# Lightning attention and a gated feed-forward layer on one core: two iotas and two additions for four small iotas, and 96 bytes of padding ahead of the tiles of q, k and v

## The chip, the core and the metric

The kernel runs on one core of a Trainium2 chip. A core has TensorE (PE; its weight loads are listed apart as PEld), VectorE (DVE), ScalarE (ACT), GpSimd (POOL) and SyncE (SP), each with its own instruction stream, and 16 DMA engines that they share. The metric is the device time of one execution in microseconds (us), the median over several runs; less is better.

## The reference

Inputs: `q`, `k`, `v` of shape (4, 8, 768, 64), eight decay factors `lam` between 0.97 and 0.99, and three weight matrices; all are float32. Linear attention with decay runs over blocks of 64 positions, and its output goes through a gated feed-forward layer:

```python
for b in range(nb):                       # 12 blocks of 64
    qb, kb, vb = q[:, :, sl], k[:, :, sl], v[:, :, sl]
    intra = einsum('bhic,bhjc->bhij', qb, kb) * Dmask        # lam ** (i - j), zero for j > i
    intra = einsum('bhij,bhjd->bhid', intra, vb)
    inter = einsum('bhid,bhde->bhie', qb * lam ** (i + 1), kv_state)
    out[:, :, sl] = intra + inter
    kv_state = lam ** 64 * kv_state + einsum('bhsd,bhse->bhde', kb * lam ** (63 - s), vb)

x = out.transpose(0, 2, 1, 3).reshape(3072, 512)
y = (sigmoid(x @ w_gate) * (x @ w_val)) @ w_out              # 512 -> 1536 -> 512
```

## The kernel before

The 768 positions are taken in six steps `n` of 128. In each step all four batches and eight heads are worked on: attention gives `XT[n]`, the transposed input of the feed-forward layer, 512 tokens wide; twelve slices `ft` of 128 hidden columns follow (`piece_gv`: products `gp` and `vp` at L484, the sigmoid at L496, the product `ht` at L499 or L501), and then four output tiles of 128 tokens (`piece_po`, L519). The attention of step n+1 is put between the slices of step n, so TensorE has the dense products to do while other engines prepare. The order on each engine is the order of the code.

Attention of step 0 has nothing to hide behind. It needs k of batches 0 and 1 (`load_hw`, issued by SP as float32 and cast at L289), the rest of k, q and v (`load`, L94, issued by POOL, float32 in memory and bf16 in the tile), transposes on TensorE (L263), products S = K Q (`piece_s`, L306), a mask (`piece_m`, L314) and products with v (`piece_a`, L337 and L580). Between them stand matrix products of zeros (L533) that nothing reads.

Memory is laid out in the order in which tiles are made, pool after pool, each tile on a multiple of 32 bytes: constants first (the weights `WG`, `WV`, `WO`, then the small tables), then the pool `qkv` (4 buffers of k, 4 of q, 5 of v, 4,096 bytes per partition each), then all others: the float32 tiles of `load_hw`, the transposed `qt` and `kt`, `kd`, `KS` and `QS`, `MT`, `XT`, `sg`, `ht`, `ob`, `st`, `xd`. The last constant is `gates` (L607), two bf16 values per partition. It ends the constants so that the first buffer of k starts at byte 64,544, which is 504 x 128 + 32; the sizes of all later tiles are multiples of 1,024, so that each of them stands 32 bytes past a multiple of 128. The weights start at byte 16,512, a multiple of 128, and so do the large masks and `lamq2`.

POOL issues the loads of q, k, v and weights, and makes the small tables between the first of them. One of these is `jn` (L132), two float32 values per partition. With s the row within a half of 64 partitions, column 0 holds -1 - s and column 1 holds 63 - s. They are filled by four iotas at L174, one for each half and column. ACT takes them as scales: `tables_late` (L217) makes `pk` (L218) and `kds` (L219), powers of `lam`, from them. `tri` (L176) follows the iotas on POOL, then the loads of q for batches 2 and 3, of v in three parts, and of the weights, slice by slice.

From step 2 on, q and k are transposed by DMA (`xbar`, L294, issued by SP). `next_loads` (L613) orders it: the two transposes, then `gate` (L609), two copies on POOL of one column of `qt` and `kt` into `gates`, which hold POOL back until both transposes have landed, then the load of v for this step and of q and k for the next. For step 2 the loads of q and k are issued by L605 and the v load by `next_loads(2)`; TensorE first reads that v in `chunk_c` (L443), behind slice 8 of step 1.

Of the kernel before, what the change touches and what calls it, by code (L numbers as in the profile page):

```python
# [9 lines left out]
BF16 = mybir.dt.bfloat16  # L10
# [6 lines left out]
def kernel(  # L17
# [11 lines left out]
    nc = tc.nc  # L29

    B, H, S, D = q.shape
    C = 128
# [9 lines left out]
    const = ctx.enter_context(tc.tile_pool(name="const", bufs=1))  # L42
# [18 lines left out]
    L = C // 2  # L61
# [20 lines left out]
    def rows_of(u):  # L82
        return slice(u * 64, (u + 1) * 64)

    def load(n, what, b0=0, b1=B):
        sl = slice(n * C, (n + 1) * C)
        for c in what:
            if (c, n) not in T_:
                T_[c, n] = qkv.tile([128, B, H, D], BF16, tag=c + "b", name=c + "b",
                                      bufs=5 if c == "v" else 4)  # L90
            src = {"q": q, "k": k, "v": v}[c]
            nat = b1 if n == 0 or c == "v" else min(b1, NB2)
            if b0 < nat:
                nc.gpsimd.dma_start(  # L94
                    out=T_[c, n][:, b0:nat],
                    in_=src[b0:nat, :, sl, :].rearrange("b h s d -> s (b h) d"))
            if nat < b1:
                m = max(nat, b0)
                for u in range(2):
                    nc.gpsimd.dma_start(  # L100
                        out=T_[c, n][:, m:b1, u::2, :],
                        in_=src[m:b1, 1 - u::2, sl, :].rearrange("b h s d -> s (b h) d"))
# [29 lines left out]
    jn = const.tile([128, 2], FP32, tag="jn")  # L132
# [31 lines left out]
    for u in range(2):  # L164
# [4 lines left out]
                            pattern=[[1, C]], channel_multiplier=-1)  # L169
    nc.gpsimd.iota(ip1, pattern=[[1, C]], base=1, channel_multiplier=0,  # L170
                   allow_small_or_imprecise_dtypes=True)
    load(0, "k", 2, 4)
    for u, i, base in ((0, 0, -1), (1, 0, -1), (0, 1, L - 1), (1, 1, L - 1)):
        nc.gpsimd.iota(jn[rows_of(u), i:i + 1], pattern=[[0, 1]], base=base, channel_multiplier=-1,  # L174
                       allow_small_or_imprecise_dtypes=True)
    nc.gpsimd.affine_select(out=tri, in_=tri, compare_op=ALU.is_gt, fill=1.0, base=0,  # L176
                            pattern=[[-1, C]], channel_multiplier=1)
# [35 lines left out]

    def powers(u):
        nc.scalar.activation(mask0[:, u], mask0[:, u], AF.Exp)

    def tables_late():  # L217
        nc.scalar.activation(pk[:, 1], lnl, AF.Exp, scale=jn[:, 0:1])  # L218
        nc.scalar.activation(kds[:, 1], lnl, AF.Exp, scale=jn[:, 1:2])  # L219
        nc.scalar.activation(pow_l, lns, AF.Exp, scale=float(L))  # L220
# [38 lines left out]
    def t_(c, n, bs, pool=ps_at, tag="ps"):  # L259
        ps = pool.tile([128, len(bs), HP, C], BF16, name="t" + c, tag=tag)  # L260
        for i, b in enumerate(bs):
            for hp in range(HP):
                nc.tensor.transpose(ps[:, i, hp, :], T_[c, n][:, b, 2 * hp:2 * hp + 2, :], ident)  # L263
        (tqs if c == "q" else tks)[n, bs[0]] = ps

    def e_q(n, bs, eng=None):
        w = len(bs)
        src = tqs[n, bs[0]] if n < FIRST_XBAR else QT[n][:, bs[0]:bs[0] + w]
        t = trsb.tile([128, 2, HP, C], BF16, tag="QS", name="QS")
        if n == 0:  # L270
            (nc.scalar.copy if eng is nc.scalar else nc.vector.tensor_copy)(t[:, :w], src)
        else:
            nc.vector.tensor_tensor(
                out=t[:, :w], in0=src,
                in1=(lamqs if swapped(n, bs[0]) else lamq).unsqueeze(1).to_broadcast([128, w, HP, C]),
                op=ALU.mult)
        for i in range(w):
            QS[n, bs[i]] = t[:, i]
# [252 lines left out]
    def zeros(m):  # L531
        for _ in range(m):
            nc.tensor.matmul(zps, lhsT=ST[1, 0][:, 0, 0], rhs=ST[1, 0][:, 0], start=True, stop=True)  # L533

    zeros(9)
    exponents(0)
    powers(0)
    cast_hw("k", 0)
    t_("k", 0, [0])
    e_k(0, [0])  # L540
    exponents(1)
    cast_hw("k", 1)
    zeros(3)
    powers(1)
    t_("q", 0, [0])
    e_q(0, [0], nc.vector)
    t_("q", 0, [1])
# [56 lines left out]
    load(1, "v", 2, 4)  # L604
    load(2, "qk")  # L605

    gates = const.tile([128, 2], BF16, tag="gates")  # L607

    def gate(n):  # L609
        for i, t in enumerate((QT[n], KT[n])):  # L610
# [157 lines left out]
```

## Time and profile before

| | |
|---|---|
| median of six runs | 226.27 us (226.12 to 227.44) |
| profiled execution | 225.77 us |
| its span on the core | 224.0 us |
| granted TensorE clock | 1.0 throughout |
| first product with weights (L484) | at 15.84 us |
| last product (L519) | 221.0 us |

The profile is of one execution, on its own time. Busy time by stretch of the span, in us, from a table of windows:

| stretch | TensorE | DVE | ACT | POOL | DMA, GB/s written |
|---|---|---|---|---|---|
| 0 to 5.7 | 4.02 | 2.67 | 3.06 | 4.35 | 113 |
| 5.7 to 8.1 | 1.47 | 1.46 | 1.93 | 2.34 | 150 |
| 8.1 to 12 | 3.26 | 2.90 | 2.89 | 3.90 | 127 |
| 12 to 17 | 4.58 | 4.40 | 3.59 | 5.00 | 168 |
| 17 to 60 | 42.73 | 24.41 | 23.60 | 23.21 | 176 |
| 60 to 78 | 17.31 | 13.42 | 10.02 | 7.84 | 151 |
| 78 to 205 | 126.84 | 51.65 | 57.20 | 17.74 | 91 |
| 205 to 224 | 15.97 | 3.31 | 4.04 | 0 | 57 |

TensorE is the busy engine from 17 us to the end; POOL is busy nearly all the time up to 17 us, mostly with issuing loads. A part of the groups of instructions (line, engine, operation, tiles, shape, count, then busy us, mean ns of one, idle time ahead and what ended it):

```profile
L484 PE MATMUL gp<-XT,WG 128*128 128x512 bf16 (+1 forms) x296 | 74.2, 374 | 0.1
L519 PE MATMUL po<-WO,ht 128*128 128x512 bf16 (+2 forms) x292 | 63.3, 370 | 0.5 <-issue 0.2
L611 POOL COPY gates<-qt 128x1 bf16<-128x1 bf16 x4 | 0.7, 186 | 49.1 <-DMA qt<-qb 49.1
L314 DVE TENSOR_TENSOR MT<-sp,mask 128x512 bf16<-128x512 f32 x16 | 9.9, 684 | 2.7 <-PE sp L306 2.7
```

The means of the first two mix shapes; with the shapes apart both are 379 ns for 128x512. Matrix products overlap in the pipeline: four of 128x512 follow each other in 0.865 us. The transposes of L294 land between 5.5 and 10.1 us after their issue for `qt`, and 4.3 to 5.0 for `kt`.

### The profile page before, as it was taken

How to read it: one execution, taken by the hardware profiler on the slowest of the kernel's cores; microseconds unless marked ns; L12 is line 12 of the kernel's file. 1: busy time of each engine (PE TensorE's matmuls, PEld its weight loads, DVE VectorE, ACT ScalarE, POOL GpSimd, SP SyncE). 2: the span in 40 equal slices, each digit the busy share in tenths (PEclk: the TensorE clock that was granted, in tenths of full speed). 3: DMA queues.
4: the chain of work that ended last, by engine and by line, in shares of the span. 5: the costliest groups of instructions: out<-in, count | busy, mean ns of one | idle time of the engine just before them, and what ended most of it. 6: DMA issues, size and time to landing. Idle time of an engine off the chain costs nothing.

```text
span 224.0 us, 5200 instructions
## 1 busy us (share of the span) xinstructions
PE 216.2 (97%) x2178; PEld 106.3 (47%) x2187; DVE 104.2 (47%) x194; ACT 106.3 (47%) x232; POOL 64.4 (29%) x85
## 2 busy tenths in 40 slices
PE   7799999999998999999999999999999999999994
PEld 2454444557444544444544444544444544444443
DVE  4686653539776700686700676700676400333300
ACT  5777534494385433376342366342367342333221
POOL 7999864760075000940291012000000000000000
PEclk9999999999999999999999999999999999999999
DMA  7999999999969999999599989212100012100022
GB/s 112 136 164 183 195 201 180 177 155 147 176 52 157 234 128 151 198 156 153 113 105 209 212 139 81 15 50 94 47 3 0 0 52 94 47 0 0 4 94 95
DMA packets 106009, 25.25 MB, mean 113 GB/s; under 512 B 97153, under 2 KB 103553, under 8 KB 105985
## 3 DMA queue, kind: packets, MB, share of 16 engines
q0 software_dynamic: 82944, 13.90, 84.2%
q1 hardware_dynamic: 22752, 10.95, 22.9%
q8 instruction: 17, 0.28, 0.6%
q10 hardware_dynamic: 288, 0.07, 0.1%
q14 instruction: 8, 0.06, 0.1%
HBM read 28.32 MB, written 6.29 MB: 154 GB/s over the span
## 4 chain that ended last, share of the span: by engine, by line
PE 67%; DMA 19%; POOL 8%; issue 2%; SPq 1%; ACT 0%; POOLq 0%
PE po L519 23%; PE gp L484 20%; PE vp L484 20%; DMA WO<-in_moe_w_out_dram 6%; DMA qb<-in_q_dram 4%; DMA WV<-in_moe_w_val_dram 4%; DMA vb<-in_v_dram 3%; POOL WV L108 2%; POOL WG L105 2%; DMA kt<-kb 2%; SPq L294 1%; POOL vb L94 1%; PE cp L443 1%; PE op L407 1%; PE op L421 1%
## 5 line engine op out<-in xcount | busy, mean ns | idle before, releaser
L484 PE MATMUL gp<-XT,WG 128*128 128x512 bf16 (+1 forms) x296 | 74.2, 374 | 0.1
L484 PE MATMUL vp<-XT,WV 128*128 128x512 bf16 (+1 forms) x292 | 74.1, 376 | 0.0
L496 ACT ACTIVATE sg<-gp 128x512 bf16<-128x512 f32 x72 | 43.0, 597 | 63.1 <-PE gp L484 63.1
L501 DVE TENSOR_TENSOR ht<-sg,vp 128x512 bf16<-128x512 bf16 x48 | 33.0, 687 | 79.9 <-PE vp L484 77.0
L519 PE MATMUL po<-WO,ht 128*128 128x512 bf16 (+2 forms) x292 | 63.3, 370 | 0.5 <-issue 0.2
L484 PEld LDWEIGHTS <-WV 128*128 128x128 bf16 x292 | 28.6, 98 | 33.4 <-DMA WV<-in_moe_w_val_dram 0.2
L519 PEld LDWEIGHTS <-ht 128*128 128x128 bf16 x300 | 28.3, 98 | 31.8
L484 PEld LDWEIGHTS <-WG 128*128 128x128 bf16 x296 | 28.1, 98 | 31.8 <-DMA WG<-in_moe_w_gate_dram 0.8
L523 ACT COPY ob<-po 128x512 f32<-128x512 f32 (+1 forms) x24 | 13.7, 572 | 38.9 <-PE po L519 38.9
L127 ACT ACTIVATE kd<-kb,kds 128x128 bf16<-128x128 bf16 (+1 forms) x88 | 28.8, 401 | 0.0
L499 DVE TENSOR_TENSOR ht<-sg,vp 128x512 bf16<-128x512 bf16 x24 | 16.5, 687 | 13.2 <-PE vp L484 13.2
L611 POOL COPY gates<-qt 128x1 bf16<-128x1 bf16 x4 | 0.7, 186 | 49.1 <-DMA qt<-qb 49.1
L94 POOL DMA_DIRECT2D vb<-in_v_dram x9 | 11.9, 1333 | 2.8 <-issue 1.7
L314 DVE TENSOR_TENSOR MT<-sp,mask 128x512 bf16<-128x512 f32 x16 | 9.9, 684 | 2.7 <-PE sp L306 2.7
L433 ACT CAST XT<-op 128x512 bf16<-128x512 f32 x16 | 8.2, 599 | 5.0 <-PE op L421 5.0
L393 DVE TENSOR_TENSOR MT<-sp,mask 128x512 bf16<-128x512 f32 x16 | 10.3, 682 | 0.0
L100 POOL DMA_DIRECT2D qb<-in_q_dram x10 | 8.8, 895 | 3.5 <-DMA WO<-in_moe_w_out_dram 3.2
L94 POOL DMA_DIRECT2D qb<-in_q_dram x8 | 8.8, 1105 | 1.7 <-POOLq L752 0.8
L100 POOL DMA_DIRECT2D kb<-in_k_dram x10 | 9.0, 917 | 1.0 <-DMA WG<-in_moe_w_gate_dram 0.6
L533 PE MATMUL zps<-st 128*128 128x512 bf16 x17 | 6.7, 530 | 1.6 <-DVE st L159 1.5
L108 POOL DMA_DIRECT2D WV<-in_moe_w_val_dram x9 | 7.3, 822 | 0.3 <-DMA WG<-in_moe_w_gate_dram 0.3
L94 POOL DMA_DIRECT2D kb<-in_k_dram x6 | 7.1, 1176 | 0.6 <-DMA WG<-in_moe_w_gate_dram 0.5
(79 smaller groups left out, 115.4 us busy)
## 6 DMA issues: line engine op xcount, KB each, us to landing
out_dram<-ob SPq DMA_DIRECT2D x19, 256.0 KB, 2.1
vb<-in_v_dram POOLq DMA_DIRECT2D x4, 512.0 KB, 7.3
qb<-in_q_dram POOLq DMA_DIRECT2D x6, 256.0 KB, 8.2
kb<-in_k_dram POOLq DMA_DIRECT2D x6, 256.0 KB, 10.7
qb<-in_q_dram POOLq DMA_DIRECT2D x12, 128.0 KB, 8.3
WO<-in_moe_w_out_dram POOLq DMA_DIRECT2D x4, 384.0 KB, 12.2
kb<-in_k_dram POOLq DMA_DIRECT2D x10, 128.0 KB, 10.7
WG<-in_moe_w_gate_dram POOLq DMA_DIRECT2D x4, 256.0 KB, 7.3
```

Of the source, the lines that this page charges most:

```text
L94: nc.gpsimd.dma_start(out=T_[c, n][:, b0:nat], in_=src[b0:nat, :, sl, :].rearrange("b h s d -> s (b h) d"))
L100: nc.gpsimd.dma_start(out=T_[c, n][:, m:b1, u::2, :], in_=src[m:b1, 1 - u::2, sl, :].rearrange("b h s d -> s (b h) d"))
L108: nc.gpsimd.dma_start(out=WV[:, :, f0 * 128:f1 * 128], in_=wv_r[:, :, f0 * 128:f1 * 128])
L127: nc.scalar.mul(KD[n][:, at, i, :], T_["k", n][:, at, i, :], kds[:, min(n // FIRST_XBAR, 1), h:h + 1])
L314: nc.vector.tensor_tensor(out=MT[n, b][:, u], in0=SP[n, b][u], in1=mask0[:, 1 - u if swapped(n, b) else u], op=ALU.mult)
L393: nc.vector.tensor_tensor(out=MT[n, bp][:, u], in0=SP[n, bp][u], in1=mask[:, u ^ bp].unsqueeze(1).to_broadcast([128, 2, HP, L]), op=ALU.mult)
L484: nc.tensor.matmul(ps[:, part], lhsT=W[:, mt, fs], rhs=XT[n][:, part, mt], start=(part is not second and mt == 0), stop=(part is not first ...
L496: nc.scalar.activation(sg, gp.rearrange("p a b -> p (a b)"), AF.Sigmoid)
L499: mul = nc.vector.tensor_mul(HT[n, ft], sg, vp.rearrange("p a b -> p (a b)"))
L501: mul = nc.vector.tensor_mul(HT[n, ft].rearrange("p (b c i) -> p c b i", b=B, c=2), sg.rearrange("p (c b i) -> p c b i", c=2, b=B), vp.rea ...
L519: nc.tensor.matmul(po[:, :c1 - c0], lhsT=HT[n, ft][:, tt * 128:(tt + 1) * 128], rhs=WO[:, ft, c0:c1], start=(ft == 0), stop=(ft == NFT - 1))
L523: (eng.copy if eng is nc.scalar else eng.tensor_copy)(o, po[:, :c1 - c0])
```

## The change

The tile `gates` is made 64 bf16 values wide, 128 bytes in place of 4; its use stays as it was. Everything behind it moves by 96 bytes, so that the first buffer of k starts at byte 64,640, which is 505 x 128, and all later tiles on multiples of 128 as well (each 128 bytes past a multiple of 256).

The four iotas for `jn` become two over all 128 partitions, one for each column, with the values -1 - p and 127 - p for partition p. That is right for column 0 in the first half and for column 1 in the second. Two additions on VectorE put the other halves right: +64 to column 0 in partitions 64 to 127, and -64 to column 1 in partitions 0 to 63 (`chunk_rows`). They stand in VectorE's order behind the cast of batch 1's k and ahead of the copy of the transposed q (L271 before). ACT's readers of `jn` wait for them in place of POOL. No other instruction changes its place on any engine.

```diff
-    for u, i, base in ((0, 0, -1), (1, 0, -1), (0, 1, L - 1), (1, 1, L - 1)):
-        nc.gpsimd.iota(jn[rows_of(u), i:i + 1], pattern=[[0, 1]], base=base, channel_multiplier=-1,
+    for i, base in enumerate((-1, C - 1)):
+        nc.gpsimd.iota(jn[:, i:i + 1], pattern=[[0, 1]], base=base, channel_multiplier=-1,
                        allow_small_or_imprecise_dtypes=True)
...
     def powers(u):
         nc.scalar.activation(mask0[:, u], mask0[:, u], AF.Exp)
+
+    def chunk_rows():
+        nc.vector.tensor_scalar_add(jn[rows_of(1), 0:1], jn[rows_of(1), 0:1], float(L))
+        nc.vector.tensor_scalar_add(jn[rows_of(0), 1:2], jn[rows_of(0), 1:2], -float(L))
...
     cast_hw("k", 1)
     zeros(3)
     powers(1)
+    chunk_rows()
     t_("q", 0, [0])
     e_q(0, [0], nc.vector)
...
-    gates = const.tile([128, 2], BF16, tag="gates")
+    gates = const.tile([128, 64], BF16, tag="gates")
```

## The prediction

> **What bounds the kernel now.** I read the page's busy table first, then the waits of TensorE, then the chain that ended last in its opening part, then a table of time windows for the DMA, then VectorE's timeline.
>
> ```profile
> PE 216.2 (97%) x2178; PEld 106.3 (47%) x2187; DVE 104.2 (47%) x194; ACT 106.3 (47%) x232; POOL 64.4 (29%) x85
> ```
>
> ```profile
> PE op L337 <- DMA vb<-in_v_dram: 0.3, 1, 0.3
> PE cp L443 <- DMA vb<-in_v_dram: 0.6, 1, 0.6
> ```
>
> TensorE is busy for 216.2 of 224.0 us. From the first gated product at 15.84 us on it has one hole over 0.2 us: L443 waits for the values of step 2, until 70.29 us, 0.64 us by the timeline. So only two places are worth anything: the opening, and whatever makes that transfer land at 70.29. The chain of waits says what stands ahead of it: POOL's issuing from 1.3 to 21.0 us, then DMA, DMA, the two transposes of L294 (54.39 to 62.4), and the load of L94 issued at 62.91. Its opening part:
>
> ```profile
> 4.71 0.17 POOL jn L174
> 4.88 0.06 issue
> 4.94 0.13 POOL jn L174
> 5.07 0.07 issue
> 5.13 0.12 POOL jn L174
> 5.26 0.05 issue
> 5.30 0.39 POOL jn L174
> 5.70 0.06 issue
> 5.76 0.31 POOL tri L176
> 6.07 1.74 POOL qb L94 x2
> 7.81 2.89 POOL vb L94 x3
> ```
>
> Start, length, what. POOL has no hole from 3.5 to 22 us, so the four small iotas delay every later load. Does the DMA feel it? The windows (PE, PEld, DVE, ACT, POOL busy, clock, DMA share, GB/s written):
>
> ```profile
> 10.00:11.50 1.50, 1.45 (x22) 1.05 (x23) 1.50 (x4) 1.17 (x5) 1.50 (x3) 1.00 1.77 99
> 11.50:13.50 2.00, 1.98 (x25) 1.01 (x23) 1.74 (x4) 1.98 (x4) 2.00 (x3) 1.00 2.41 154
> 15.00:19.00 4.00, 3.90 (x28) 2.15 (x29) 3.47 (x10) 2.28 (x6) 4.00 (x7) 1.00 1.81 179
> 24.00:30.00 6.00, 6.00 (x30) 2.74 (x28) 3.20 (x7) 2.21 (x4) 4.51 (x6) 1.00 1.45 196
> 32.00:34.00 2.00, 2.00 (x11) 0.89 (x10) 1.29 (x2) 0.60 (x1) 0.87 (x1) 1.00 1.24 206
> 43.00:49.00 6.00, 5.95 (x39) 3.03 (x38) 2.79 (x5) 4.39 (x11) 4.64 (x5) 1.00 2.44 156
> ```
>
> The q, k and v loads run at 154 to 156 GB/s wherever they have work, but at 99 between 10.0 and 11.5 us, just before the transfers issued at 7.81 come in. The DMA starves there for (156-99)/156 x 1.5 = 0.55 us; the same sum over 7.5 to 8.5 us (140 GB/s) gives 0.10 more. After 11.5 us its rate belongs to the packet size, so it is full until 49 us: what is saved before 11.5 us reaches the transposes, the load and TensorE's hole undiminished.
>
> **The change part by part.** *Four iotas become two.* By the chain the third and fourth with the gaps ahead of what follows are 0.12 + 0.05 + 0.39 + 0.06 = 0.62 us. The new ones cover 128 partitions in place of 64; the gate copies (L611, 128x1, 186 ns) and the first iota (0.17) say that partitions cost nothing, so I leave 0.17 and 0.13. tri then starts at 5.13, and qb's two issues at 5.44 in place of 6.07; no other queue is passed, and three DMAs of n=0's v and all weights move with them. The DMA regains the smaller of 0.62 and its starvation of 0.65: 0.62 us. At least 0.05: the fourth iota was held up, and what did it may hold tri:
>
> ```profile
> 5.23 0.42 DVE L289 CAST kb<-h 128x512 bf16<-128x512 f32 x1
> 6.66 0.50 DVE L289 CAST kb<-h 128x512 bf16<-128x512 f32 x1
> 8.56 0.42 DVE L271 COPY QS<-tq 128x512 bf16<-128x512 bf16 x1 [1.40 <-PE tq L263]
> ```
>
> The iota that took 0.39 ends at 5.69, right after this cast at 5.65. tri would come at 5.13, ahead of the cast at 5.23, and I take it that the first one goes on; else tri runs from 5.70 and 0.06 is left. If the cast waits for tri instead (0.2 us), its transposes on PE end 0.2 later, but ACT takes them only at 6.54, 0.2 or more after they are done: nothing.
>
> *Two additions on VectorE.* They stand behind the second cast and ahead of the copy at 8.56. Nearest rows: 0.15 us (L223, 64x8) and 0.16 (L226); at least 0.11 (the memset of L158), at most 0.49 (L225, a copy of 64x8 that ended with a POOL issue at 17.37). Two are 0.22 to 0.98, I take 0.32. They wait for iotas done at 5.07, and lie in DVE's idle 1.40 us, so they cost nothing. Behind them queue the QS copy and the mask products, for which PE waits; without that cover 0.32 would reach them, and still only eat the 0.64 us that TensorE has in hand at 70 us. ACT's pk and kds (L218, L219) now wait for DVE, at 9.74 us, over 1 us later. If each addition stops POOL's issuing while it runs, 0.32 of the 0.62 is lost.
>
> *Addresses.* The gate tile grows from 4 to 128 bytes; all pools behind it move by 96 bytes, from 32 past a multiple of 128 to 128 past a multiple of 256, where the weights already lie (WG starts at byte 16,512). For the engines the rows of before hold both kinds. L484 streams XT (moves) and L519 streams WO (does not): 379 ns each. Weight loads of WG and ht: 98 and 98. DVE: L242, all on aligned tiles, 685 ns against L314's 684; L585 682 against L350's 688. ACT: 391 for L198 and for L127. A difference of 6 ns over 194 DVE instructions is 1.2 us, all in an engine that idles half the time: nothing.
>
> For loads, time per packet and engine is 16 x bytes / rate: 22.9 ns for 256 bytes (15 to 19 us), 41.8 for 512, 79.5 for 1024, all weights at the new alignment. Their slope, (79.5-22.9)/768 = 0.074 ns per byte, puts 128 bytes at 13.4 ns; the q, k, v packets at the old one take 16 x 128 / 156 = 13.1. So there is no penalty to lift. I take 0; both ends are 0.3 ns for 34,816 packets up to 70 us (10+12+12 batches of 1024), over 16 engines: 0.65 us down or up.
>
> Transposes read 256-byte rows of qb and kb, 2048 each. Their peak is 257 GB/s (61 to 62 us), 15.9 ns a row. No row shows them at another address; the nearest, 13.1 and 22.9 ns, over 2 x 128 rows per engine bound it by -0.7 and +1.8 us. Since they mostly run below that peak (L294's issue took 3.21 and 3.11 us for the first two, kt's 1.38 in the median) I take 0.
>
> [...]
>
> Sum: -0.62 in the DMA chain. TensorE can follow: the last products on v(0) (15.32) wait for v, while their masks are ready at 14.75 (L314), so its path moves by up to 0.5 and the hole keeps about 0.5. Against the profiled execution, 225.77 us with 224.0 of span and 1.77 around it, this is 225.15; against the median of 226.27, which lies 0.50 above, 225.65.
>
> **The rivals.** *Packets get cheaper too.* For it: q, k, v are 34,816 packets on the chain. Against it: the straight line through the weights. With 0.3 ns less the chain gains 0.62 + 0.65 = 1.27, but TensorE allows 0.5 + 0.64 = 1.14: 225.15.
>
> *The gain is given back.* tri waits for the cast, or the dip at 10 us is no lack of descriptors. For it: the iota's hold-up by the cast, and that the rate also sags at 49 to 55 us (149 GB/s), where POOL issues nothing. Against it: such a sag is 4%, the dip 37%, and it ends when the transfer issued at 7.81 can come in. 0.06 is left: 226.2.
>
> *Slower: the transposes.* Place: 54.39 to 62.4 us, ahead of the v load that TensorE waits for. Price: up to 1.8 less 0.62 gives 227.45. It decides from 0.62 us for both together, and shows as slower from 1.3. Against it: they are held up by more than their reading.
>
> **How the numbers follow.** Chances: forecast 0.46, cheaper packets 0.23, given back 0.17, transposes 0.14. About 0.3% (0.68 us) is what a measurement of this kernel tells from no change: 225.59 and 226.95. The forecast lies just inside the first, so a scatter of 0.2 between medians puts nearly half of it, 0.21, beyond. Faster 0.21 + 0.23 = 0.44; same 0.25 + 0.17 + 0.01 = 0.43; slower 0.13. The forecast's own range is 225.3 to 226.0. The whole range goes from 224.9, the rival's 225.15 less 0.25 of scatter between medians, to 227.0, which leaves out the dearer half of the transposes.
>
> **What would show it.** Two iotas on POOL, tri at 5.13 us, qb's issue near 5.45; 10.0 to 11.5 us near 150 GB/s; the first gp near 15.4; L443 still waiting about 0.5 us for vb, near 69.7; packet rates of 156 GB/s and gp, po rows of 379 ns unchanged. It is wrong if tri or the first WG issue (10.65) does not move, if the dip stays, or if the first two transposes take other than 8.0 us together.

## The result, and the profile after

| | before | changed |
|---|---|---|
| median, all runs of the two | 226.36 us (46 runs, 225.72 to 227.52) | 224.83 us (22 runs, 224.41 to 225.28) |
| ratio, with its 95% interval | | 0.9926 (0.9916 to 0.9936) |
| profiled execution, span | 225.77, 224.0 us | 224.87, 223.1 us |
| first product with weights | 15.84 us | 15.41 us |
| first product on v of step 2 (L443, now L447) | 70.29 us | 69.40 us |

The change gains 0.7%, some 1.5 us by the medians, where 0.6 was forecast. In two later groups, each beside the kernel before on one chip, it gained 1.2 us by the medians (E12: 225.99 to 224.78; E15: 226.00 to 224.81). The measured 224.83 lies just under the range that was given.

The chain of waits of the changed kernel in the opening (start, length, what):

```profile
4.72 0.23 POOL jn L174 x2
4.95 0.25 POOL tri L176
5.20 1.84 POOL qb L94 x2
7.04 2.89 POOL vb L94 x3
```

The q loads are issued at 5.20 us in place of 6.07, so POOL gained 0.87 us, more than the 0.62 that the rows of before gave. The waits of TensorE still name the v of step 2, with half the time:

```profile
PE gp L488 <- ACT XT L588: 0.3, 1, 0.3
PE cp L447 <- DMA vb<-in_v_dram: 0.3, 1, 0.3
```

That is one execution. In two more profiles of the same kernel (E12 and E15) this wait is not listed; the first product with weights comes at 14.95 and 15.17 us there, and TensorE then waits at 17.7 and 17.9 us for the weights `WV`. E12:

```profile
PE vp L488 <- DMA WV<-in_moe_w_val_dram: 0.6, 1, 0.6
```

So a time from one profile says little about differences of half a microsecond in the opening.

The table of windows of the changed kernel (busy time of PE, PEld, DVE, ACT, POOL; clock; DMA share, which is the time of all packets in flight, so it can be above 1; GB/s):

```profile
10.00:11.50 1.50, 1.22 (x14) 0.61 (x12) 1.33 (x3) 1.19 (x3) 1.50 (x3) 1.00 2.45 156
11.50:13.50 2.00, 2.00 (x28) 0.92 (x27) 1.43 (x3) 1.98 (x3) 2.00 (x3) 1.00 2.39 156
49.00:55.00 6.00, 5.84 (x125) 4.39 (x123) 5.49 (x14) 3.49 (x9) 0.00 (x0) 1.00 2.46 159
```

The dip at 10 us (99 GB/s) is gone. And something moved that was not forecast: the last window. There the kernel before has

```profile
49.00:55.00 6.00, 5.84 (x135) 4.64 (x136) 5.00 (x12) 3.66 (x10) 0.00 (x0) 1.00 3.35 149
```

POOL issues nothing in this stretch, and E1 below, which has the two iotas and the old addresses, is as slow there. Fewer bytes arrive, while the share of the DMA is higher by a third: each packet is in flight for longer. In the trace's packet records the 128-byte packets of q, k and v take 32 ns nearly throughout; in the kernel before, 6% of them take 40 ns or more, most of these between 8.75 and 10.25 and between 49 and 55 us, where they are 35% and 46% of all. In the changed kernel 0.2% do.

### The profile page after: what moved, and what is told of

Read it like the earlier page. It is cut to its first block, busy times and chain, and to the rows that moved or that the text cites. A ratio compares the mean times of both kernels' runs of the same rounds, so it can differ in the third digit from the quotient of the medians.

```text
span 223.1 us, 5199 instructions
## 1 busy us (share of the span) xinstructions
PE 216.0 (97%) x2178; PEld 106.1 (48%) x2187; DVE 104.5 (47%) x196; ACT 106.3 (48%) x232; POOL 63.9 (29%) x83
## 4 chain that ended last, share of the span: by engine, by line
PE 67%; DMA 20%; POOL 10%; issue 1%; ACT 0%; POOLq 0%; SPq 0%
PE po L523 23%; PE gp L488 20%; PE vp L488 20%; DMA WO<-in_moe_w_out_dram 6%; DMA kb<-in_k_dram 4%; DMA WV<-in_moe_w_val_dram 4%; DMA vb<-in_v_dram 3%; POOL WV L108 2%; POOL WG L105 2%; DMA kt<-kb 2%; POOL vb L94 1%; PE cp L447 1%; PE op L411 1%; PE op L425 1%; POOL kb L94 1%
## 5 line engine op out<-in xcount | busy, mean ns | idle before, releaser
L503 DVE TENSOR_TENSOR ht<-sg,vp 128x512 bf16<-128x512 bf16 x24 | 16.5, 687 | 13.5 <-PE vp L488 13.3
```

The source lines that it names most:

```text
L503: mul = nc.vector.tensor_mul(HT[n, ft], sg, vp.rearrange("p a b -> p (a b)"))
```

## The experiments

Two theories stood against each other. *Issue*: all of the gain is POOL's earlier issue, and the kernel before merely often waits longer at L443 than its profile shows. *Addresses*: at 32 bytes past a multiple of 128, stretches of the q, k and v packets are slow. Each group below was run on one chip beside the kernel before; ratios are to that.

**One half of the change at a time (E1, E2).** E1 is the changed kernel with the old gate tile:

```diff
-    gates = const.tile([128, 64], BF16, tag="gates")
+    gates = const.tile([128, 2], BF16, tag="gates")
```

> The two iotas and two additions, with the gate tile at 4 bytes, so all addresses as before. If earlier issue on POOL is all of the gain and the kernel before merely has runs with a longer wait at L443 than its profile shows: about 1.5 us less than before (ratio 0.993), and little scatter. If the issue is worth what the two profiles show and the addresses bring the rest: 0.6 to 0.9 less (0.996 to 0.997), and the scatter of before (1.8 us between fastest and slowest) stays.

E2 is the kernel before with the gate tile 64 wide, and nothing else.

> Only the gate tile at 128 bytes, with the four iotas. If addresses cost nothing: 226.3, ratio 1.000 within 0.001, scatter as before. If the old addresses slow some packets (VectorE and DMA in the stretch from 49 to 55 us, 149 against 159 GB/s): 0.6 to 0.9 less, ratio 0.996 to 0.997, and a narrower scatter.

Measured: E1 226.44 us, ratio 1.0023 (1.0012 to 1.0034). E2 225.05 us, 0.9965 (0.9951 to 0.9979). The iotas alone gain nothing; they lose a little. The addresses alone bring 0.9 us (225.93 to 225.05) of the 1.2 to 1.5, and the two together more than the sum. Neither theory explains the gain alone: the issue is not the gain by itself, and yet the rest of the gain needs it. First a window of the kernel before, then windows of E1 and its wait at L447:

```profile
8.50:10.00 1.50, 0.96 (x21) 0.70 (x20) 0.90 (x2) 1.22 (x4) 1.50 (x3) 1.00 2.84 147
```

```profile
8.50:10.00 1.50, 1.50 (x19) 1.16 (x16) 0.42 (x1) 0.81 (x2) 1.50 (x3) 0.50 3.00 151
10.00:11.50 1.50, 1.30 (x19) 0.99 (x16) 1.27 (x3) 0.76 (x4) 1.50 (x3) 0.50 3.61 148
11.50:13.50 2.00, 1.98 (x25) 1.26 (x23) 1.62 (x4) 2.00 (x4) 2.00 (x3) 1.00 3.52 147
49.00:55.00 6.00, 6.00 (x134) 4.28 (x133) 4.56 (x11) 3.96 (x11) 0.00 (x0) 1.00 3.39 147
```

```profile
PE cp L447 <- DMA vb<-in_v_dram: 1.2, 1, 1.2
```

The dip is filled, as the prediction said (148 in place of 99). But now packets are slow all the way from 8.5 to 13.5 us, 147 to 151 GB/s with a share of 3.0 to 3.6. The kernel before was slow from 8.75 to 10.25 us only, and ran at 154 with 2.41 from 11.5 on. The loads of v for step 0 show what becomes of the saving: E1 issues them 0.73 us earlier (7.06 in place of 7.79 us), and from issue to landing they take, first before, then in E1:

```profile
DMA to landing us min/median/max: 5.5/5.6/5.8
```

```profile
DMA to landing us min/median/max: 6.2/6.2/6.4
```

So they land 0.04 to 0.12 us earlier. The changed kernel, which differs from E1 in the addresses alone, issues them at 7.03 and has them 0.5 to 0.6 us before E1. E1's first weights land at 15.85 us, against 15.79 before and 15.37 in the changed kernel, and its first product with weights comes at 16.03. That product may be late by the clock too: this execution had a granted clock of 0.50 from 8.1 to 11.5 us, and the median product that transposes k (L267) took 304 ns, against 219 before. The wait at L447 grows to 1.2 us. But ten of E1's twelve runs had a clock of 0.998 or 1.0 and took as long (226.1 to 227.2 us), so the clock is not what E1 lost. In E2 the same stretch from 49 us reads

```profile
49.00:55.00 6.00, 6.00 (x136) 4.63 (x136) 5.01 (x12) 3.79 (x11) 0.00 (x0) 1.00 2.43 157
```

and the wait at L443 is not listed any more.

**Which tiles (E6, E7).** A pool that nothing uses, made behind the pool `qkv`, shifts only what comes after it. E6 leaves q, k, v where they were and puts the rest on multiples of 128; E7 does the reverse (with the gate tile 64 wide and a pad of 16).

```diff
     qkv = ctx.enter_context(tc.tile_pool(name="qkv", bufs=5))
+    padp = ctx.enter_context(tc.tile_pool(name="padp", bufs=1))
     hwp = ctx.enter_context(tc.tile_pool(name="hwp", bufs=2))
...
+    padp.tile([128, 48], BF16, tag="pad", name="pad")
```

> Four iotas, q, k and v 32 bytes past a multiple of 128 as before, all later pools (float32 k, transposed q and k, and the rest) on multiples of 128. If the load packets into q, k and v make the difference: as before, ratio 1.000 within 0.0015. If the transposes' targets or the engines' tiles make it: 0.9965.

> The reverse: q, k and v on multiples of 128, all later pools 32 bytes past. If the load packets make the difference: ratio 0.9965, as with all addresses moved, no wait at L443. If the others make it: 1.000.

Measured: E6 226.24 us, 1.0007 (0.9995 to 1.0019); E7 225.13 us, 0.9967 (0.9954 to 0.9981). From 49 to 55 us, first E6, then E7:

```profile
49.00:55.00 6.00, 6.00 (x131) 4.00 (x130) 4.55 (x8) 4.36 (x12) 0.53 (x1) 1.00 3.43 148
```

```profile
49.00:55.00 6.00, 6.00 (x136) 4.52 (x131) 5.27 (x13) 3.80 (x10) 0.00 (x0) 1.00 2.44 157
```

So it is the tiles of q, k and v that matter. All other moved tiles, with everything that the engines do in them, cost nothing at the old addresses that the time of E6 or E7 shows.

**Which address (E5, E3, E14).** E5 makes the gate tile 32 wide, so that later tiles start 64 bytes past a multiple of 128 (four iotas). E3 and E14, the same kernel, make it 128 wide with two iotas: multiples of 256.

> Four iotas, the gate tile at 64 bytes: later tiles start 64 past a multiple of 128, so half of the 128-byte packets of q, k and v still cross a line of 256 bytes, but each starts on a multiple of 64. If crossing a 256-byte line is what slows them: as before (ratio 1.000 within 0.0015), slow packets from 49 to 55 us (under 150 GB/s). If a start off a multiple of 64 is what slows them: as the kernel with addresses alone, ratio 0.9965, 157 GB/s there.

> The changed kernel with the gate tile at 256 bytes, so that every later tile starts on a multiple of 256 and no packet of 128 or row of 256 bytes crosses such a line. If crossing costs something in loads or transposes: below the changed kernel by 0.1 to 0.5 us, the first two transposes under 8.0 us together. If not: 224.8, as the changed kernel.

> Two iotas and multiples of 256, beside the changed kernel on one chip. If multiples of 256 bring more than multiples of 128: 0.3 to 0.4 below the changed kernel, as the two groups before suggest. If that was a difference of chips: equal within 0.15.

Measured: E5 225.82 us, 1.0001 (0.9987 to 1.0014), with 147 GB/s and a share of 3.54 from 49 to 55 us. So a start on a multiple of 64 is not enough. At 32 and at 64 past, every 128-byte packet crosses a multiple of 128 and every second one a multiple of 256; at 128 and 256 none crosses either. No run here tells which of the two crossings costs the time, or whether it is the crossing itself.

E3 224.42 us, 0.9937 (0.9922 to 0.9952), beside E4's 224.83 on its chip, where the changed kernel itself was not run; E14 224.52, 0.9935 (0.9922 to 0.9948), beside the changed kernel's 224.81 (E15: 0.9945, 0.9932 to 0.9958). Twice 0.3 to 0.4 us lower, but the intervals overlap. The expected sign of it, shorter transposes, is not there: from the issue of the first transpose to the landing of the second it is 8.4 us in E3 as in the changed kernel.

> The changed kernel as their measure: ratio 0.9925 to 0.9945.

**What the iotas are worth at good addresses (E8), and whether issuing still limits (E4).** E8 is E3 with the four iotas. E4 is the changed kernel with `tri` made behind the last v load of step 0.

> All later tiles on multiples of 256, four iotas. If the wait at L443 is gone on these addresses, the opening alone decides, and the two iotas are worth the 0.58 us by which the first product with weights came earlier (15.97 against 15.39): 0.6 above the kernel with two iotas on 256 (ratio to before 0.9963 against 0.9937). If they are worth nothing: the same as that one, 0.9937.

> The changed kernel with the mask tri made on POOL behind the last v load of step 0, so that the q and v loads are issued another 0.3 us earlier. If the DMA is full from 5.5 us on in the changed kernel: no gain, 224.8 within 0.2. If issuing still limits the opening: 0.2 to 0.3 less, 224.5.

Measured: E8 225.04 us, 0.9967 (0.9945 to 0.9990), 0.5 to 0.6 us above E3 and E14, though the intervals overlap at their ends; two of its twelve runs, at a granted clock of 0.991, took 227.1 and 227.2. On multiples of 128, the addresses of the change, four iotas took 225.05 and 225.13 us (E2, E7) and two 224.78 to 224.83: the iotas are worth 0.2 to 0.4 us there. The 0.58 us of the expectation came from one profile each, and that is not firm: E8's own first product with weights comes at 16.47 us. Over all profiles the first weights land at 15.7 to 16.8 us with four iotas, at either address, at 15.8 to 15.9 with two on the old addresses (E1, E10, E16), and at 14.9 to 15.8 with two on the new.

E4 224.83 us, 0.9955 (0.9941 to 0.9969), beside 224.83 of the changed kernel over all its runs: no gain. In the changed kernel an issue earlier by another 0.3 us is worth nothing more; its DMA moves 145 to 156 GB/s all the time from 5.5 to 13.5 us.

**Is the wait at L443 the way to the end? (E9 to E12).** The state products of step 2 and their updates go one slice later, where the v load has 1.7 us more:

```diff
-                more[8].append(do(chunk_c, nx, bp, cs))
+                more[8 + late].append(do(chunk_c, nx, bp, cs))
...
-                more[8].append(do(update_0, nx, bp))
+                more[8 + late].append(do(update_0, nx, bp))
...
-                    more[9 + bp].append(do(update_1, nx, bp))
+                    more[9 + late + bp].append(do(update_1, nx, bp))
```

> The kernel before, with the state products of step 2 (L443, chunk_c) and the two updates that follow them moved behind slice 9 of step 1 in place of slice 8, 1.7 us later, so that the v load has that much more time. If the wait at L443 is what the old addresses cost: ratio to before 0.9965, as with the addresses moved (225.0 to 225.2), though the packets stay as slow as before. If the addresses act elsewhere: 1.000.

> Two iotas on the old addresses, with the same products a slice later. If the iotas gained nothing there because the DMA chain to L443 sets the end: now 0.995 or lower, 0.2 to 0.6 us below the previous one. If slow packets also hold up the opening there (first product with weights at 16.03 in that profile): the same as the previous one, or up to 0.2 above.

> The changed kernel with the same products a slice later. If its wait of 0.3 us at L443 is the last thing that the DMA chain costs it: 0.3 below the changed kernel, 224.5, as on multiples of 256.

> The changed kernel beside these on one chip, as their measure: ratio 0.993 to 0.9955.

Measured: E9 225.37 us, 0.9965 (0.9951 to 0.9979), the ratio of E2 to the last figure, while its packets stay slow:

```profile
49.00:55.00 6.00, 6.00 (x134) 4.30 (x133) 4.56 (x11) 3.91 (x11) 0.00 (x0) 1.00 3.45 147
```

So what the addresses alone bring is that wait. A second sign of it: from the first product with weights to the end of the last product the profile of the kernel before has 205.19 us, that of E9 204.36, those of E2 and E7 204.35. Where both the addresses and the later products are in, it is no less (E11 204.36, E13 204.47), so the two are one gain and not two.

E10 225.37 us, 0.9958 (0.9940 to 0.9975): with the wait out of the way the iotas still gain nothing that can be told from E9 on the old addresses. That slow packets hold up the opening fits this (window 11.5 to 13.5: 147 GB/s, share 3.52), but both profiles are of executions with a clock of 0.50 from 8.3 to 11.7 us, and it is not shown. E11 224.56, 0.9929 (0.9911 to 0.9948) against E12, the changed kernel, 224.78, 0.9931 (0.9912 to 0.9950): 0.2 lower where 0.3 was expected, and not beyond the intervals.

**Both together (E13).** Multiples of 256, two iotas, and the later state products.

> Two iotas, all later tiles on multiples of 256, and the state products of step 2 a slice later. If the wait at L443 was all that remained behind the opening: the same as on 256 without the move, 224.4 to 224.5, since that profile showed no wait there. If its timed runs often had one: up to 0.2 lower.

Measured 224.53 us, 0.9935 (0.9921 to 0.9949), the same as E14. The opening is what is left. E3, E11, E13 and E14 all lie at 224.4 to 224.6; none is shown to beat the changed kernel's 224.8 beyond its interval.

**What ends a slow stretch (E16).** On the old addresses with two iotas, POOL's small tables stand between the q and the v loads, with two repeats of the iota into `ip1`, to let the DMA run dry for a moment.

> Two iotas on the old addresses, but jn and tri, and two repeats of an earlier iota, stand on POOL between the q and the v loads of step 0, so that the DMA runs dry there for up to 0.5 us. If a full queue keeps slow packets slow and a pause ends them, as the kernel before suggests: 8.5 to 10 us slow (DMA share near 3), a dip at 10 to 11.5, and from 11.5 to 13.5 us quick packets again (share 2.4, 152 GB/s or more). If the pause has nothing to do with it: share near 3.5 and 147 GB/s from 11.5 to 13.5, as without the pause.

Measured: 227.39 us, 1.0051 (1.0028 to 1.0074), windows:

```profile
10.00:11.50 1.50, 0.40 (x8) 0.23 (x8) 0.78 (x2) 1.50 (x4) 1.50 (x3) 0.94 3.09 143
11.50:13.50 2.00, 1.80 (x21) 1.60 (x22) 1.67 (x3) 1.23 (x5) 2.00 (x3) 0.50 3.02 144
```

The pause did not come about: no dip, and no quick stretch either, with 146 GB/s and a share of 3.03 from 8.5 to 10 us, 143 to 144 and 3.02 to 3.09 after it. So the run decides nothing on its question. What it lost against E1 goes with the clock: the opening came late (first product with weights at 18.18 us, though the first weights had landed at 15.80), TensorE stood idle (0.40 of 1.5 us busy in the first window), and its granted clock fell to 0.50 in the second. Of its eight timed runs the two with a granted clock of 1.0 took 226.2 us, the six with 0.983 to 0.992 took 227.3 to 228.6.

## Why the prediction was wrong

*What bounds the kernel* was right: the opening and the wait at L443. E9 shows the wait to be worth 0.35%, E8 beside E3 and E14 the opening some 0.3% on multiples of 256.

*Four iotas become two*: the mechanism was right, and the size too small. 0.62 us was the sum of four rows of before; measured 0.87, since the two iotas took 0.23 together in place of the 0.36 of the old first two with their gap, tri follows with no gap, and it takes 0.25 in place of 0.31. That tri would come ahead of the cast was right (4.95 against 5.27). That the dip was a lack of descriptors fits E1 and the changed kernel, where it is gone (148 and 156 GB/s in place of 99). But its depth does not follow the issue alone: E2 issues as the kernel before and has 139 GB/s in that window, E16 issues v at 7.81 us as before and has 143.

*"What is saved before 11.5 us reaches the transposes, the load and TensorE's hole undiminished"*: this failed on the old addresses. The term of -0.62 us measured +0.5 there (E1 226.44 against 225.93): the loads of v are issued 0.73 us earlier and land 0.04 to 0.12 earlier, in a stretch of slow packets. At the new addresses 0.2 to 0.6 us arrive (E2, E7 and E8 against their pairs with two iotas).

*The additions*: two rows of 0.15 us, at 7.33 and 7.51, 0.30 against 0.32, ahead of the QS copy, which waited for TensorE behind them. Nothing, as forecast.

*Addresses on the engines*: right. gp and po rows are 380 ns against 379, weight loads 98, the mask products 682 and 683 against 682 and 684; E6 confirms it by time.

*"So there is no penalty to lift"*: this is the step that failed. The line through the weights was compared with the packets of q, k and v from 43 to 49 us, a stretch in which they are quick at any address: all these kernels have 155 or 156 GB/s there. A mean over one stretch was taken for a property of the address. The reading that these loads run at 154 to 156 GB/s wherever they have work was wrong: from 8.5 to 10 us the kernel before has 147 GB/s with a share of 2.84. The other window that showed the opposite, 49 to 55 us at 149 GB/s with a share of 3.35 against 2.44, was read, but as a sag without a cause, and used only in a rival. The addresses alone are worth 0.35%, 0.9 us by the medians (E2), where 0 was taken.

*The cap of 1.14 us* (226.27 less it is 225.13, where 225.15 was written) was too low: three groups gave 1.2 to 1.5 us between the medians. It rested on the 0.64 us hole of one execution that ran 0.5 us below the median of its kernel. In E1's profile the wait is 1.2 us, in E6's 0.7. How it varies over the runs of before was not traced.

*The transposes* took other than the 8.0 us together that were forecast: from the first issue to the second landing 8.1 us before, 8.4 after, 8.4 on multiples of 256, and 8.1 in E6, whose targets are moved and whose sources are not. All profiles on multiples of 128 or 256 have 8.4, those on the old addresses 8.1 or 8.2, but E9 8.3. Whether the addresses of the sources cost these 0.3 us, or what else the DMA does beside the transposes, no run separates.

The rival *Packets get cheaper too* was what happened. Its price of 0.65 us for the addresses was somewhat low (0.9), and its reason against, the straight line, was wrong.

## What to carry to other kernels

A mean rate from one stretch does not clear a cost that comes in stretches: compare the share of the DMA with its bytes, window by window, and ask about every window where the share is high and the rate low. Of two edits for one chain, one can be worth nothing alone and something beside the other; try each alone before it is credited. Where packets of 128 bytes fill the DMA, try their tiles where no packet crosses a multiple of 128 bytes: it brought 0.35% here for 124 bytes.

## What the runs showed of the hardware

Loads that write 128 bytes a packet ran at 155 or 156 GB/s from 43 to 49 us at any address. From 49 to 55 us, at 32 or 64 bytes past a multiple of 128, they ran at 147 to 149 GB/s with a DMA share of 3.35 to 3.54, and in the kernel before 46% of the packets took 40 ns and longer in place of 32. What starts such a stretch, and what ends it, was not found; at multiples of 128 or 256 it did not occur in any of eleven profiles (154 to 160 GB/s there with a share of 2.34 to 2.47; in the changed kernel under 1% of such packets).

In four profiles (E1, E6, E9, E10) the granted clock of TensorE stood at 0.50 for 3.4 us, from 8.1 or 8.3 us on, and in E16 from 11.3 to past 13.5. In these five TensorE was busy for 0.33 to 0.43 of 1.0 us from 7.5 to 8.5. Of the other thirteen only the kernel before was as idle there (0.38), and it had been busy for 1.52 of 2.0 us from 5.5 to 7.5, where E1 and E16 have 1.04; E5 has 0.50 from 7.5 to 8.5, the rest 0.92 to 0.97. That the idle time costs the clock is argued from this alone. In E16 the runs at a lower clock were 1 us or more longer than those at 1.0; E1's, 226.57 and 226.81 at 0.992, lie close to its median of 226.44.

In E16 a piece of POOL's work ran longer beside a cast on VectorE, though it had started first: tri ran from 6.61 to 7.36 us, 0.75 in place of 0.31, with the cast of batch 1's k from 6.80 to 7.21 inside it. The prediction took it that the first one goes on; E16 speaks against it, and in the changed kernel this was not put to the test, since tri was done before the cast began.
